# Attention's token-wide products computed in two column halves of the array, beside the state update

## The chip, the cores and the metric

The kernel runs on one core of one Trainium2 chip. The metric is the device time of one execution in microseconds (us); a run gives one time, and the number compared is the median over runs.

## What is computed

Three stages follow each other: an RWKV-like attention, a mixture of eight experts with Sinkhorn gates, and a mixture of eight experts in which each token takes its best one. The change is in the first stage and in two gate products.

```python
def _attn_ref(r, k, v, w, u):            # B=2, H=8 heads, S=768 tokens, D=48
    state = zeros((B, H, D, D))
    for t in range(S):
        cur = einsum('bhd,bhe->bhde', u[None] * kt, vt)
        y[:, :, t] = einsum('bhd,bhde->bhe', rt, state + cur)
        state = wt[:, :, :, None] * state + einsum('bhd,bhe->bhde', kt, vt)
    return y

def _moe_ref(x, w_gate, w1, w2):         # N=1536 tokens, 384 wide, E=8, F=1024
    P = exp(x @ w_gate - max)
    ...                                  # 8 rounds: rows and columns of P scaled
    for e in range(E):
        out += P[:, e:e + 1] * (maximum(x @ w1[e], 0) @ w2[e])

def _moe2_ref(x, expert_emb, tau, w1, w2):
    logits = normalised(x) @ normalised(expert_emb).T / tau
    expert_idx = argmax(logits, axis=1)
    ...                                  # the chosen expert's output, times its softmax weight
```

## The kernel before, in words

The 1536 tokens are 12 chunks of 128, six for each of the two batches. Attention works chunk by chunk in steps, each a Python function that a letter stands for:

- `a` (`att1a`, L579 to L584, VectorE): running products of the decay, and `Rh`, the scaled `r`.
- `b` (`att1b`, L592, L597, VectorE): products from the other side, and `Kt`, the scaled `k`; then loads for the chunk after next.
- `c` (`att1c`, L604 to L609): the part of a token with itself, `bv`; VectorE and, at the end, GpSimd.
- `d` (`att2`): on TensorE the token-by-token products of `Kt` and `Rh` (L620, on two row halves) and four transposes of `Kt` (L623); then VectorE masks them into `AT` (L625), ScalarE copies `KtT` (L630), GpSimd makes `T`, the decayed old state (L633).
- `f` (`att3`): the output of the chunk in one PSUM bank `y`. Four products of `Rh` with `T` (L643, the old state; not in chunks 0 and 6), 96 columns each, and eight of `AT` with the values (L649), 48 columns each; 128 tokens are the stationary columns of both. VectorE adds `bv` into `x` (L655).
- `z` (`att3z`): the state update, eight products of 48 by 48 (L678) that alternate between the lower and the upper column half of the array; VectorE puts them into `S` (L683, L685). The last chunk of a batch, 5 and 11, has no such products.
- `g` (`att4`): three transposes of `x` (L690) and its copies for the experts (L692 to L695).
- `h` (`att5`): three products of the chunk with the gate's weights (L729), eight columns each; ScalarE copies them into `P` (L730).

There is no scheduler: instructions stand on each engine in the order in which the Python code issues them. `run` issues the pieces of an expert unit one by one, and after piece i the steps that stand in slot i of a hand-written string, slots being parted by commas (L1261 to L1264 with the units, the strings' chunks 3 to 11). A unit of 256 tokens has eight hidden pieces (`h_piece`: nine products at L272, ScalarE's `hh`, VectorE's `hl`) and then four output pieces (`y_part`, twelve products each at L292 to L294). Chunks 0 to 2 run before, between the first expert's first chunk and short runs of idle products (`warm`, L522) that keep TensorE busy.

In the third stage `route_mm` (L884) makes three products of a transposed token tile with the expert embeddings, for the tiles 10 and 11 alone.

An fp32 product at these lines is recorded twice, as two weight loads and two multiplies.

Of the kernel before, what the change touches and what calls it, by code (L numbers as in the profile page):

```python
# [19 lines left out]
def rwkv_sinkhorn_moe_top1_moe(  # L20
# [17 lines left out]
    nc = tc.nc  # L38
    B, CPB, _, _, H, D = rkv.shape
    NT, DM = out.shape  # L40
    E, _, FF = m1w1.shape
    NTILE = NT // 128
    KD = DM // 128
# [22 lines left out]
    def ps():  # L66
        return psp.tile([128, 512], F32, tag="ps", name="ps")
# [19 lines left out]
    enT = const.tile([128, KD, E], F32, name="enT")  # L87
    wtab = const.tile([128, E], F32, name="wtab")
    first = const.tile([128, 1], I32, name="first")
# [25 lines left out]
    def xT_of(t0, n):  # L115
        i, o = (0, t0) if t0 < TL else (1, t0 - TL)
        return [t[:, :, o * 128:o * 128 + n] for t in xT_t[i]]
# [179 lines left out]
    def unit_pieces(g, xh, xl, n, finish, nq=2):  # L297
        hts, box = [], []
        pieces = [lambda f=f: h_piece(g, f, xh, xl, n, hts) for f in range(KF)]
        for tl in range(n // 128):  # L300
            for q in range(nq - 1):
                pieces.append(lambda tl=tl, q=q: y_part(g, q, nq, tl, hts, box))

            def last(tl=tl):
                finish(tl, y_part(g, nq - 1, nq, tl, hts, box))

            pieces.append(last)
        return pieces
# [209 lines left out]
    def warm(n):  # L518

        t = ps()  # L520
        for _ in range(n):
            nc.tensor.matmul(t[:, 0:128], oneb, oneb)  # L522
# [18 lines left out]
    Tt = nat.tile([128, HP, 2 * D], F32, name="T")  # L541
    wg8 = acc[0:E, NTILE - 1, 0:DM]
    wgT = nat.tile([128, KD, E], F32, name="wgT")
# [91 lines left out]
    def att3(c):  # L635
        d = st[c]
        first = c % CPB == 0
        vv = vn[c % NB]
        y = ps()
        begin = True  # L640
        if not first:
            for p in range(HP):
                nc.tensor.matmul(  # L643
                    y[:, p * 2 * D:(p + 1) * 2 * D], d["Rh"][0:64 + D, p, :], Tt[0:64 + D, p, :],
                    start=begin, stop=False,
                )
                begin = False
        for h in range(H):
            nc.tensor.matmul(  # L649
                y[:, h * D:(h + 1) * D], d["AT"][:, h % 2, h // 2, :], vv[:, h, :],  # L650
                start=begin, stop=(h == H - 1),
            )
            begin = False
        x = a1.tile([128, DM], F32, tag="x", name="x")
        nc.vector.tensor_tensor(x, y[:, 0:DM], flat(d["bv"]), ALU.add)  # L655
        d["x"] = x
        v_read(c)

    def v_read(c):
        st[c]["reads"] = st[c].get("reads", 0) + 1  # L660
        if st[c]["reads"] == 2:
            att_load_rows(c + NB)
# [61 lines left out]
    def att5(c):  # L724

        xf = st.pop(c)["xf"]
        p = ps()
        for j in range(KD):
            nc.tensor.matmul(p[:, 0:E], xf[:, j, :], wgT[:, j, :], start=(j == 0), stop=(j == KD - 1))  # L729
        nc.scalar.activation(out=P[:, c, :], in_=p[:, 0:E], func=AF.Copy)  # L730


# [43 lines left out]
    def m1_finish(e, t0):  # L776
        def f(tl, p):
            t = t0 + tl
            a = acc[:, t, 0:DM]
            if e == 0:  # L780
                nc.scalar.activation(out=a, in_=p, func=AF.Copy)
            else:
                if e == 1:
                    nc.scalar.mul(a, a, P[:, t, 0:1])
                nc.vector.scalar_tensor_tensor(
                    out=a, in0=p, scalar=P[:, t, e:e + 1], in1=a, op0=ALU.mult, op1=ALU.add
                )
        return f
# [3 lines left out]
    def m1_unit(e, t0, n, nq=2):  # L792
        return unit_pieces(e, *xT_of(t0, n), n, m1_finish(e, t0), nq)
# [86 lines left out]
    def route_mm(t):  # L880
        xT = rr.pop(t)
        p = ps()
        for j in range(KD):
            nc.tensor.matmul(  # L884
                p[:, 0:E], xT[:, j * 128:(j + 1) * 128], enT[:, j, :], start=(j == 0), stop=(j == KD - 1)
            )
        nc.vector.tensor_copy(lg[:, t, :], p[:, 0:E])

    def route_arg(t0, t1):
# [261 lines left out]
    with tc.manual_schedule():  # L1151
# [61 lines left out]
        p = ps()  # L1213
# [8 lines left out]
        split_lo(0, 0)  # L1222
        warm(W2)
        att3(0)
        split_hi(0, 1)
        split_lo(0, 1)
# [12 lines left out]
        def att(text):  # L1239

            steps = {
                "a": att1a, "b": att1b, "c": att1c, "d": att2, "f": att3, "z": att3z, "g": att4, "h": att5,
            }
            return [[lambda w=w: steps[w[0]](int(w[1:])) for w in slot.split()] for slot in text.split(",")]

        def run(pieces, sides):
            for pc, sd in zip(pieces, sides):
                pc()
                for it in sd:
                    it()  # L1250

        def both(x, y):
# [3 lines left out]
            att("a1, b1, z0, h0, , d1, , b2 g1 z1 h1"),  # L1256
            [[gate_T], [], [hi(3), lo(3, nc.gpsimd)], [hi(4), lo(4, nc.gpsimd)], [hi(5)], [hi(6), lambda: warm(W3)],
             [lambda: att1c(1), lo(5), lo(6), lambda: att1a(2), lambda: att3(1)], []],
        ))
        run([lambda: warm(W4)] * 4, att("d2 c2 a3, z2, f2, g2"))  # L1260
        run(m1_unit(0, 1, 256), att("b3, c3 h2, d3, a4, f3, z3 b4, g3 c4, d4 h3, a5, f4, b5, g4 c5 z4"))  # L1261
        run(m1_unit(0, 3, 256), att("d5 h4, a6, f5, z5 b6, g5 c6, h5, d6, a7, f6, z6 b7, g6 c7, h6"))
        run(m1_unit(0, 5, 256), att("d7, a8, f7, z7 b8, g7 c8, h7, d8, a9, f8, z8 b9, g8 c9, d9 h8"))
        run(m1_unit(0, 7, 256), att("a10, f9, z9 b10, g9 c10, d10 h9, a11, f10, z10 b11, g10 c11, d11, f11, g11 z11 h10"))  # L1264
        att_stack.close()
        seven = ExitStack()
        sp0 = ctx.enter_context(tc.tile_pool(name="sp0", bufs=1, side="left", reuse_waits="tile"))
# [6 lines left out]
        h2 = seven.enter_context(tc.tile_pool(name="h2", bufs=4, side="left", reuse_waits="tile"))  # L1274
# [9 lines left out]
        def route(t0, t1, eng):  # L1284
# [12 lines left out]
        S0 = row_sums(0, nc.vector)  # L1297
        run(m1_unit(0, 9, 384, 4), [
            [lambda: att5(NCH - 1), sk[0]] + S0[0:1], [sk[1]] + S0[1:2], [sk[2], sk[3]] + S0[2:4], S0[4:5],
            [sk[4]] + S0[5:6], [sums(0)], [sk[5]] + S0[6:7], [w1[0]] + S0[7:8],  # L1300
            [sk[6]], [], [sums(1)], [sk[7]], [], [w1[1]],
# [109 lines left out]
        def more_stages():  # L1411
            stage[:0] = [flat(en)[:, i * FF:(i + 1) * FF] for i in range(E * DM // FF)]
            load_to(E + SURE)

        m2_slot(0, [
            (0, [lambda: route_mm(10), lambda: route_tr(11), ra[4], more_stages]), (1, [lambda: route_mm(11), ra[5], rb[0], rb[1]] + its[6:7]),
            (3, rb[2:4]), (4, rb[4:]), (5, [lambda: m2_load(1)]), (6, [lambda: m2_load(2)]),
            (10, [overflow]), (14, [lambda: m2_xT(1)]),
# [55 lines left out]
```

## Time and profile before

| | |
|---|---|
| median of 3 runs | 1069.5 us (1069.35 to 1069.74) |
| the profiled execution | 1068.51 us, span 1066.8 us |
| TensorE busy | 1046.4 us, 98% of the span |
| VectorE, ScalarE, GpSimd | 66%, 39%, 19% |
| mean granted TensorE clock | 0.995 |
| attention | from the start to about 175 us of the span |

The span is what the profile covers; the execution's own time has 1.7 us around it. In the profile PE is TensorE's multiply, PEld its weight load, DVE is VectorE, ACT ScalarE, POOL GpSimd and SP the engine that issues most transfers. A group of records is written as one row with its count (x16); its busy time is the union of its records, and the time in brackets is how long the engine had stood idle before it, with what ended that.

### The profile page before, as it was taken

How to read it: one execution, taken by the hardware profiler on the slowest of the kernel's cores; microseconds unless marked ns; L12 is line 12 of the kernel's file. 1: busy time of each engine (PE TensorE's matmuls, PEld its weight loads, DVE VectorE, ACT ScalarE, POOL GpSimd, SP SyncE). 2: the span in 40 equal slices, each digit the busy share in tenths (PEclk: the TensorE clock that was granted, in tenths of full speed). 3: DMA queues.
4: the chain of work that ended last, by engine and by line, in shares of the span. 5: the costliest groups of instructions: out<-in, count | busy, mean ns of one | idle time of the engine just before them, and what ended most of it. 6: DMA issues, size and time to landing. Idle time of an engine off the chain costs nothing.

```text
span 1066.8 us, 17966 instructions
## 1 busy us (share of the span) xinstructions
PE 1046.4 (98%) x6833; PEld 1029.2 (96%) x6833; DVE 702.7 (66%) x1404; ACT 414.8 (39%) x857; POOL 202.3 (19%) x387
## 2 busy tenths in 40 slices
PE   8899999999999999999999999999999999999996
PEld 8899999999999999999999999999999998999996
DVE  7777785766665565566556645655566788987774
ACT  3122223353532343234333323432434545566553
POOL 2210115113010011001000200000144664143111
PEclk9899999999999999999999999999999999999999
DMA  9433220110021022012101101201010314977762
GB/s 258 133 86 93 68 68 2 60 60 1 30 92 66 31 87 99 1 61 60 30 1 54 50 16 30 60 30 60 16 61 1 112 53 142 307 251 240 260 216 89
DMA packets 55774, 91.57 MB, mean 86 GB/s; under 512 B 5355, under 2 KB 47191, under 8 KB 55554
## 3 DMA queue, kind: packets, MB, share of 16 engines
q1 hardware_dynamic: 53056, 85.60, 25.7%
q0 software_dynamic: 2624, 4.75, 1.2%
q8 instruction: 56, 0.92, 0.4%
q14 instruction: 36, 0.29, 0.1%
q10 hardware_dynamic: 2, 0.00, 0.0%
HBM read 80.42 MB, written 13.28 MB: 88 GB/s over the span
## 4 chain that ended last, share of the span: by engine, by line
PE 70%; issue 14%; DVE 7%; POOL 5%; ACT 3%; DMA 1%; POOLq 0%; SPq 0%; DVEq 0%; ACTq 0%
PE ps L499 28%; PE ps L424 24%; PE ps L272 6%; PE ps L649 2%; PE ps L292 2%; PE ps L294 1%; PE ps L293 1%; PE ps L620 1%; POOL tmp L721 1%; DVE ps L714 1%; POOL xs L1090 1%; PE ps L643 1%; POOL out_dram L1136 1%; PE ps L623 1%; DVE keep L435 1%
## 5 line engine op out<-in xcount | busy, mean ns | idle before, releaser
L499 PE MATMUL ps<-wA,hh 128*128 128x384 f32 x864 | 221.5, 337 | 0.4 <-ACT hh L439 0.4
L499 PEld LDWEIGHTS ps<-wA,hh 128*128 128x128 f32 x864 | 156.7, 188 | 1.0 <-ACT hh L439 1.0
L503 DVE SCALAR_TENSOR_TENSOR acc<-ps,Pe,acc 128x384 f32<-128x384 f32 x144 | 88.7, 616 | 101.9 <-PE ps L499 101.4
L430 ACT ACTIVATE keep<-ps 128x384 f32<-128x384 f32 x144 | 70.3, 489 | 209.5 <-PE ps L424 207.7
L499 PE MATMUL ps<-wA,hl 128*128 128x384 f32 x432 | 145.7, 337 | 0.1
L440 DVE SCALAR_TENSOR_TENSOR hl<-keep,hh 128x384 fp32r<-128x384 f32 x144 | 81.5, 566 | 92.1 <-ACT hh L439 92.1
L435 DVE TENSOR_TENSOR keep<-ps,keep 128x384 f32<-128x384 f32 x192 | 106.3, 554 | 41.1 <-PE ps L424 35.1
L230 POOL TENSOR_TENSOR stage<-stage 128x128 f32<-128x128 f32 x96 | 49.6, 538 | 415.3 <-DMA stage<-in_moe_w_dram 413.4
L439 ACT ACTIVATE hh<-keep 128x384 fp32r<-128x384 f32 x144 | 75.6, 525 | 123.7 <-DVE keep L435 123.6
L277 ACT ACTIVATE hh<-ps 128x256 fp32r<-128x256 f32 (+1 forms) x152 | 61.9, 410 | 125.6 <-PE ps L272 121.5
L424 PE MATMUL ps<-xTAhi,wA 128*128 128x384 f32 x396 | 101.7, 338 | 0.2 <-ACT keep L430 0.2
L292 PE MATMUL ps<-wA,hh 128*128 128x384 f32 x264 | 90.4, 342 | 0.1
L278 DVE SCALAR_TENSOR_TENSOR hl<-ps,hh 128x256 fp32r<-128x256 f32 (+1 forms) x152 | 67.7, 455 | 33.6 <-ACT hh L277 30.7
L294 PE MATMUL ps<-wA,hl 128*128 128x384 f32 x264 | 88.5, 335 | 0.0
L293 PE MATMUL ps<-wA,hh 128*128 128x384 f32 x264 | 88.3, 335 | 0.0
L499 PEld LDWEIGHTS ps<-wA,hl 128*128 128x128 f32 x432 | 81.1, 188 | 1.3 <-DVE hl L440 1.3
L256 DVE TENSOR_TENSOR wA<-stage,wA 128x768 fp32r<-128x768 f32 (+2 forms) x65 | 72.7, 1124 | 5.4 <-ACT wA L250 5.0
L499 PE MATMUL ps<-slot,hh 128*128 128x384 f32 x288 | 74.2, 339 | 0.0
L424 PEld LDWEIGHTS ps<-xTAhi,wA 128*128 128x128 f32 x396 | 71.7, 188 | 0.5 <-ACT keep L430 0.5
L250 ACT ACTIVATE wA<-stage 128x768 fp32r<-128x768 f32 (+2 forms) x65 | 60.2, 958 | 25.8 <-POOL stage L230 25.1
L424 PE MATMUL ps<-xTAlo,wA 128*128 128x384 f32 x198 | 66.7, 337 | 0.0
L272 PE MATMUL ps<-xTAhi,wA 128*128 128x256 f32 (+1 forms) x336 | 59.3, 312 | 0.7 <-ACT xTAhi L692 0.6
(312 smaller groups left out, 2133.0 us busy)
## 6 DMA issues: line engine op xcount, KB each, us to landing
stage<-in_moe_w_dram SPq DMA_DIRECT2D x55, 384.0 KB
stage<-in_moe_w_dram SPq DMA_DIRECT2D x19, 512.0 KB
en<-in_moe_w_dram SPq DMA_DIRECT2D x17, 512.0 KB
stage<-in_moe_w_dram SPq DMA_DIRECT2D x28, 256.0 KB
rkv<-in_rkv_dram SPq DMA_DIRECT2D x12, 576.0 KB
en<-in_moe_w_dram SPq DMA_DIRECT2D x18, 384.0 KB
rk<-in_wrk_dram SPq DMA_DIRECT2D x24, 192.0 KB
stage<-in_moe_w_dram SPq DMA_DIRECT2D x28, 128.0 KB
```

The source lines that it names most:

```text
L256: eng.tensor_tensor(out=lo, in0=src, in1=hi.bitcast(F32), op=ALU.subtract)
L272: nc.tensor.matmul(p[:, 0:n], w1_of(g, kk, f)[lo], b[:, kk, :], start=(i == 0), stop=(i == len(mm) - 1))
L292: nc.tensor.matmul(p, hh[:, ts], w2h, start=(f == 0), stop=False)
L293: nc.tensor.matmul(p, hh[:, ts], w2l, start=False, stop=False)
L294: nc.tensor.matmul(p, hl[:, ts], w2h, start=False, stop=(f == KF - 1))
L424: nc.tensor.matmul(t, w, x, start=first_mm and q == 0, stop=q == n - 1, skip_group_check=True,)
L430: nc.scalar.activation(out=t, in_=st_[i][bank][:, 0:384], func=AF.Copy)
L435: nc.vector.tensor_tensor(t, st_[i][bank][:, 0:384], t, ALU.add)
L439: nc.scalar.activation(out=hh, in_=src, func=AF.Relu)
L440: nc.vector.scalar_tensor_tensor(out=hl, in0=src, scalar=0.0, in1=hh.bitcast(F32), op0=ALU.max, op1=ALU.subtract)
L499: nc.tensor.matmul(p, h[:, ts], w, start=n == 0, stop=n == len(mm) - 1)
L503: nc.vector.scalar_tensor_tensor(out=a, in0=p, scalar=P[:, t, e:e + 1], in1=a, op0=ALU.mult, op1=ALU.add)
```

## The change

The output, old-state, gate and route products keep their operands and their sums. Each is now issued as two products, one for the tokens 0 to 63 and one for the tokens 64 to 127, whose results go to the lower and the upper 64 partitions of the bank, that is, to the two column halves of the array. In the order strings of chunks 3 to 11 the state update `z` and the gate product `h` of the chunk before move into the slot of an output `f`, right behind it.

```diff
         y = ps()
-        begin = True
+        halves = [slice(64 * j, 64 * j + 64) for j in range(2)]
         if not first:
             for p in range(HP):
+                for s in halves:
+                    nc.tensor.matmul(
+                        y[s, p * 2 * D:(p + 1) * 2 * D], d["Rh"][0:64 + D, p, s], Tt[0:64 + D, p, :],
+                        start=(p == 0), stop=False,
+                    )
+        for h in range(H):
+            for s in halves:
                 nc.tensor.matmul(
-                    y[:, p * 2 * D:(p + 1) * 2 * D], d["Rh"][0:64 + D, p, :], Tt[0:64 + D, p, :],
-                    start=begin, stop=False,
+                    y[s, h * D:(h + 1) * D], d["AT"][:, h % 2, h // 2, s], vv[:, h, :],
+                    start=(first and h == 0), stop=(h == H - 1),
                 )
-                begin = False
-        for h in range(H):
-            nc.tensor.matmul(
-                y[:, h * D:(h + 1) * D], d["AT"][:, h % 2, h // 2, :], vv[:, h, :],
-                start=begin, stop=(h == H - 1),
-            )
-            begin = False
...
         for j in range(KD):
-            nc.tensor.matmul(p[:, 0:E], xf[:, j, :], wgT[:, j, :], start=(j == 0), stop=(j == KD - 1))
+            for i in range(2):
+                s = slice(64 * i, 64 * i + 64)
+                nc.tensor.matmul(p[s, 0:E], xf[:, j, s], wgT[:, j, :], start=(j == 0), stop=(j == KD - 1))
...
         for j in range(KD):
-            nc.tensor.matmul(
-                p[:, 0:E], xT[:, j * 128:(j + 1) * 128], enT[:, j, :], start=(j == 0), stop=(j == KD - 1)
-            )
+            for i in range(2):
+                nc.tensor.matmul(
+                    p[64 * i:64 * i + 64, 0:E], xT[:, j * 128 + 64 * i:j * 128 + 64 * i + 64], enT[:, j, :],
+                    start=(j == 0), stop=(j == KD - 1),
+                )
...
-        run(m1_unit(0, 1, 256), att("b3, c3 h2, d3, a4, f3, z3 b4, g3 c4, d4 h3, a5, f4, b5, g4 c5 z4"))
-        run(m1_unit(0, 3, 256), att("d5 h4, a6, f5, z5 b6, g5 c6, h5, d6, a7, f6, z6 b7, g6 c7, h6"))
-        run(m1_unit(0, 5, 256), att("d7, a8, f7, z7 b8, g7 c8, h7, d8, a9, f8, z8 b9, g8 c9, d9 h8"))
-        run(m1_unit(0, 7, 256), att("a10, f9, z9 b10, g9 c10, d10 h9, a11, f10, z10 b11, g10 c11, d11, f11, g11 z11 h10"))
+        run(m1_unit(0, 1, 256), att("b3, c3, d3, a4, f3 z3 h2, b4, g3 c4, d4, a5, f4 z4 h3, b5, g4 c5"))
+        run(m1_unit(0, 3, 256), att("d5, a6, f5 z5 h4, b6, g5 c6, , d6, a7, f6 z6 h5, b7, g6 c7, "))
+        run(m1_unit(0, 5, 256), att("d7, a8, f7 z7 h6, b8, g7 c8, , d8, a9, f8 z8 h7, b9, g8 c9, d9"))
+        run(m1_unit(0, 7, 256), att("a10, f9 z9 h8, b10, g9 c10, d10, a11, f10 z10 h9, b11, g10 c11, d11, f11 h10, g11 z11"))
```

How the strings move the instructions is seen at two places. The first is TensorE around the output of chunk 3, the first in such a unit: L272 is a hidden piece, L729 the gate product of chunk 2, L620 and L623 step `d` of chunk 3, L643 and L649 its old state and output, L678 its state update. Before:

```order
L729 MATMUL ps<-wgT,acc 128x8 x3
L272 MATMUL ps<-xTAhi,wA 128x256 x6
L272 MATMUL ps<-xTAlo,wA 128x256 x3
L620 MATMUL ps<-Rh,Kt 128x128 x8
L623 MATMUL ps<-ident,Kt 128x128 x4
...
L643 MATMUL ps<-T,Rh 128x96 x4
L649 MATMUL ps<-rkv_132,AT 128x48 x8
L272 MATMUL ps<-xTAhi,wA 128x256 x6
L272 MATMUL ps<-xTAlo,wA 128x256 x3
L678 MATMUL ps<-rkv_132,KtT 48x48 x8
```

In the changed kernel:

```order
L272 MATMUL ps<-xTAhi,wA 128x256 x6
L272 MATMUL ps<-xTAlo,wA 128x256 x3
L620 MATMUL ps<-Rh,Kt 128x128 x8
L623 MATMUL ps<-ident,Kt 128x128 x4
...
L644 MATMUL ps<-T,Rh 64x96 x8
L650 MATMUL ps<-rkv_132,AT 64x48 x16
L678 MATMUL ps<-rkv_132,KtT 48x48 x8
L731 MATMUL ps<-wgT,acc 64x8 x6
L272 MATMUL ps<-xTAhi,wA 128x256 x6
```

The gate product no longer stands ahead of L620, and output, state update and gate are one block of column halves, with twice as many products at the first and the last.

The second place is VectorE around the state update of chunk 4: L655 is its `x`, L685 the state's copy into `S`, L592 and L597 make `Kt` of chunk 5, L605 and L607 belong to its step `c`.

```order
 L655 TENSOR_TENSOR x<-ps,bv 128x384
+L685 TENSOR_TENSOR S<-ps,T 48x4x48 x2
 L592 SCALAR_TENSOR_TENSOR suf<-w_135,seg 128x516
 L597 TENSOR_TENSOR Kt<-rk_130,suf 128x512
...
 L605 TENSOR_TENSOR rkv_132<-rkv_132 128x384
 L607 TENSOR_REDUCE b<-rkv_132 128x8
-L685 TENSOR_TENSOR S<-ps,T 48x4x48 x2
 L278 SCALAR_TENSOR_TENSOR hl<-ps,hh 128x256
```

The copy into `S` moves ahead of the next chunk's `Kt`. In the other chunks of that stretch it moves ahead of one `hl` (L278) and stood ahead of `Kt` before. On SP one load of rows goes ahead of the two pairs of loads for `w` and `rk` of a chunk.

## Rows read from the trace of the kernel before

**Rows 1.** The page, part 1: busy us (share of the span) and instructions.
```profile
PE 1046.4 (98%) x6833; PEld 1029.2 (96%) x6833; DVE 702.7 (66%) x1404; ACT 414.8 (39%) x857; POOL 202.3 (19%) x387
```

**Rows 2.** Busy time by stage: stretch, its us, engines, granted clock, DMA, GB/s.
```profile
53.00:175.00 122.00, 120.93 (x1058) 115.92 (x1058) 87.97 (x175) 30.24 (x77) 20.27 (x67) 1.00 0.24 69
81.60:96.90 15.30, 15.30 (x145) 14.76 (x144) 13.48 (x28) 4.98 (x13) 2.46 (x3) 1.00 0.38 116
39.00:45.80 6.80, 6.80 (x62) 6.23 (x61) 4.61 (x9) 0.60 (x1) 2.52 (x2) 0.50 0.59 161
```

**Rows 3.** TensorE's longest wait in total: for whom, us, times, longest one.
```profile
PE ps L690 <- DVE x L655: 2.2, 2, 2.1
```

**Rows 4.** Records of five lines: count, ns min/median/max, first and last start us.
```profile
L643 PE MATMUL ps<-T,Rh x80: 246/275/474, 29.2 to 167.0; 112*128 112x96 f32 x80
L649 PEld LDWEIGHTS ps<-rkv,AT x192: 187/192/192, 13.8 to 168.7; 128*128 128x128 f32 x192
L729 PEld LDWEIGHTS ps<-wgT,acc x72: 186/192/192, 23.4 to 174.3; 128*128 128x128 f32 x72
L884 PEld LDWEIGHTS ps<-enT,xT x12: 186/192/192, 890.8 to 893.4; 128*128 128x128 f32 x12
L678 PEld LDWEIGHTS ps<-rkv,KtT x160: 119/125/196, 22.6 to 157.7; 128*48 128x48 f32 x160
```

**Rows 5.** Weight loads in order of time, 59 to 75 us: start, busy us, instruction.
```profile
62.14 0.44 PEld L678 LDWEIGHTS ps<-rkv,KtT 128*48 128x48 f32 x16
72.95 1.87 PEld L649 LDWEIGHTS ps<-rkv,AT 128*128 128x128 f32 x16
```

**Rows 6.** Multiplies of two lines, columns as in rows 4.
```profile
L678 PE MATMUL ps<-rkv,KtT x160: 208/208/316, 22.6 to 157.7; 128*48 128x48 f32 x160
L1214 PE MATMUL ps<-u_sb,ones x2: 481/533/585, 6.4 to 6.8; 1*128 1x384 f32 x2
```

**Rows 7.** TensorE in order of time, 57 to 64 us, chunk 3's output and state.
```profile
57.20 0.87 PE L272 MATMUL ps<-xTAhi,wA 128*128 128x256 f32 x6
...
58.27 1.07 PE L643 MATMUL ps<-T,Rh 112*128 112x96 f32 x8
...
60.90 0.96 PE L272 MATMUL ps<-xTAhi,wA 128*128 128x256 f32 x6
...
62.15 0.56 PE L678 MATMUL ps<-rkv,KtT 128*48 128x48 f32 x16
...
63.81 0.49 PE L690 MATMUL ps<-ident,x 128*128 128x128 f32 x3
```

**Rows 8.** Order of time at chunk 1's `x` and its transposes.
```profile
35.53 0.55 DVE L655 TENSOR_TENSOR x<-ps,bv 128x384 f32<-128x384 f32 x1
...
36.14 0.55 PE L690 MATMUL ps<-ident,x 128*128 128x128 f32 x3 [2.05 <-DVE x L655]
```

**Rows 9.** Order of time at chunk 0's `x`.
```profile
15.89 0.56 DVE L655 TENSOR_TENSOR x<-ps,bv 128x384 f32<-128x384 f32 x1 [0.49 <-PE ps L649]
```

**Rows 10.** Order of time from the gate of chunk 2 to `d` of chunk 3.
```profile
52.56 0.73 PE L729 MATMUL ps<-wgT,acc 128*128 128x8 f32 x6
...
53.14 0.95 PE L272 MATMUL ps<-xTAhi,wA 128*128 128x256 f32 x6
...
53.71 0.69 DVE L597 TENSOR_TENSOR Kt<-rk,suf 128x512 f32<-128x512 f32 x1
...
54.55 1.16 PE L620 MATMUL ps<-Rh,Kt 48*128 48x128 f32 x16
```

**Rows 11.** Order of time at chunk 10: its `AT` and its output.
```profile
151.93 1.28 DVE L625 TENSOR_TENSOR AT<-ps,mask 128x512 f32<-128x512 f32 x2
...
153.56 1.03 PE L643 MATMUL ps<-T,Rh 112*128 112x96 f32 x8
```

**Rows 12.** Order of time at chunk 6: its `Kt` and its `d`.
```profile
92.00 0.69 DVE L597 TENSOR_TENSOR Kt<-rk,suf 128x512 f32<-128x512 f32 x1
...
94.24 0.94 PE L620 MATMUL ps<-Rh,Kt 48*128 48x128 f32 x12
```

## The prediction

> **What bounds the kernel now.** I read the engine totals first: TensorE is busy 98% of the span, VectorE 66% [rows 1], so time leaves this kernel only where TensorE gets less to do and nothing else takes its place. The table by stage comes next: between 53 and 175 us, where chunks 3 to 11 of attention run inside the first expert's products, TensorE is busy 120.93 of 122.00 us and VectorE 87.97; in a stretch where the first expert's hidden pieces run (81.6 to 96.9 us) VectorE has 13.48 of 15.30; from 39.0 to 45.8 us the granted clock is 0.50, the 1.2 GHz level [rows 2]. The list of TensorE's waits is short: at its head stand 2.2 us in all for `x` [rows 3]. So a microsecond taken from attention's products is a microsecond of the kernel, except where one of those waits, or one just behind it, swallows it.
>
> **What a product costs.** Each fp32 product is two records, a weight load and a multiply each. The old-state line has 80 records, the output line 192, the gate line 72, the route's line 12 [rows 4]. The output line loads 128 columns of weights per record; its 16 loads last 1.87 us together, one load 0.192, so they follow each other every (1.87 − 0.192) / 15 = 0.1119 us, though only 48 columns move through. The state update, before and after on 48-column halves, has 16 loads in 0.44 us, one lasting 0.125: eight pairs, one every (0.44 − 0.125) / 7 = 0.0450 us [rows 4, 5]. Two points give 0.836 ns per weight column, so a pair of 64-column halves should come every 0.0584 us if the load sets the pace. After the change every record of 128 columns is one such pair: 0.0535 us less.
>
> The multiply sets the pace where more columns move. An fp32 record lasts 481 ns with 384 moving columns (the shorter of two) and 208 with 48 [rows 6]: 0.81 ns per column. A state-update pair (48 moving) is then 39 + 6 ns; the old-state pair (96 moving) 78 + 6 = 84 ns. The trace shows no old-state pair: 58.4 ns (load alone) and 84 ns (multiply) are its ends, 111.9 the present; I take 84, because the two multiply rows are of this data type. Gain 0.0279.
>
> - Output: 192 × 0.0535 = 10.27 us.
> - Gate: 72 × 0.0535 = 3.85 us. Route: 12 × 0.0535 = 0.64 us.
> - Old state: 80 × 0.0279 = 2.23 us (4.28 at the other end).
>
> Together 17.0 us. The Trainium skill (TensorE: Matmul & The Clock Gate, section Part 3: Packing small matmuls) gives a measured 2.38 times for three column tiles; the same yield per tile would be 1.59 times for two, a pair every 70.4 ns, and by that estimate the sum would be 13.7 us, not 17.0. The state update's pairs in this trace, 45.0 ns, do not show such a loss.
>
> **What entering and leaving the halves costs.** Two hidden pieces with a state update between them take 60.90 to 63.81 = 2.91 us; the same piece alone takes 57.20 to 58.27 = 1.07 [rows 7]. The update costs 2.91 − 2.14 = 0.77, of which eight pairs are 0.36: 0.41 us per block of halves. A state update already pays this; output and gate put beside it pay nothing more. New blocks are those that do not touch a state update: output of chunks 0, 1, 2; gate of 0 and 11; the route's products of tiles 10 and 11; and the blocks of chunks 5 and 11, which have no state product. Nine × 0.41 = 3.69 us. That leaves 13.3 us.
>
> **What of it is on the path.** Three places give it back:
> - Output of chunk 1, with its old state, gets 16 × 0.0535 + 8 × 0.0279 − 0.41 = 0.67 us shorter, but its `x` starts at 35.53 with VectorE at work without a pause before it, and TensorE stands 2.05 us for it [rows 8]. Minus 0.67. Chunk 0's gain stays: there `x` waited for TensorE [rows 9].
> - Gate 2 now runs at 52.56 to 53.14, ahead of a product that starts at 54.55 when `Kt` (53.71 + 0.69) is ready [rows 10]. Moved behind output 3, it no longer covers that wait: minus 0.6, the 0.58 it filled.
> - Gate 9 leaves the place before output 10, whose `AT` is ready only 0.35 us ahead (151.93 + 1.28 against 153.56) [rows 11]: minus 0.4. The same with gate 4 before output 5, where the room is larger: minus 0.2.
>
> Other moves I cost at nothing. The state's copy into `S`, 0.71 us of VectorE, now comes ahead of a `hl` and, for chunk 4, ahead of the next `Kt`; but its product also ends a piece earlier, and `Kt` 6 was ready at 92.69 for a product at 94.24, 1.55 us of room [rows 12]. Without that room each such move costs 0.71. The gate's 0.18 us copy on ScalarE has nobody waiting before the normalisation. One row load on SP goes ahead of two others; the chunk that reads it is two chunks away. But TensorE leaves about 11 of the 122 us of this stage while VectorE keeps its 88, so its share goes from 72% to 79%; I put 0.6 us on small new waits. The bounds of this term are 0 and the second rival below.
>
> Sum: 13.3 − 0.7 − 0.6 − 0.6 − 0.6 = 10.8 us. The profiled execution took 1068.5 us, a span of 1066.8 and 1.7 around it; less 10.8 it is 1057.7. The median of the runs shown, 1069.5, is 1.0 above it, so the median after is **1058.7 us**. Old state at its good end and no new waits give 1069.5 − 10.8 − 2.05 − 0.6 = 1056.0; if half the price of a block were the tail of the work before it, 1.8 less: 1054.2.
>
> **The rivals.**
> 1. *VectorE becomes the bound in the hidden-piece stretches.* For: 13.48 of 15.30 us [rows 2], and TensorE's work there shrinks by over 1 us. Against: the 1.55 us of room [rows 12], and VectorE starts such a stretch with work ahead of it. Outputs 3, 5, 7, 9 and 10 lie in such stretches; each block's 0.86 + 0.22 + 0.32 = 1.4 us would turn into waits, 7.0 in all, instead of the 1.8 I took off for waits and moved gates there: 1058.7 + 5.2 = 1063.9. Chance 0.15.
> 2. *The low clock lasts longer.* It stood at 0.50 for 6.8 us [rows 2], after TensorE had idled 2.05 us and worked thinly [rows 8]; that idle time grows by 0.67. A second stretch as long would do 3.4 us of full-clock work in 6.8: 1058.7 + 3.4 = 1062.1. Against: some of that stretch waits for VectorE anyway. Chance 0.10.
> 3. *Slower: the two halves of one product load one after the other.* They share their moving operand, which the state update's halves do not. Then a pair takes 2 × 58.4 = 116.8 ns: 276 × 4.9 ns = 1.35 us more for output, gate and route; the old state 2 × 84 = 168 ns, 80 × 56 ns = 4.5 more; with 3.69 for the blocks, 9.5 us: 1079. It decides from about 96 ns a pair, where 356 × 16 ns no longer pays the blocks and the 1.9 us of covered places. Against: 45.0 ns for a pair of 48 columns is what one load takes by the per-column rate, so two ran at once [rows 5]. Chance 0.05. The Trainium skill (same page and section) states a rule that points this way: a weight load overlaps a running multiply only if it uses other rows of the array, and both halves use the same rows. The trace does not agree for 48 columns; no run here shows 64.
> 4. *No change:* switching costs 1.5 us a block where new, not 0.41, and nine of them eat the 13.3 + 3.69 − 1.9 us: about 1068. The state update inside hidden pieces speaks against it [rows 7]. Chance 0.04.
>
> **How the numbers follow.** My forecast has 0.66 (own range 1054.8 to 1061). The range reaches over rival 2 and about half of rival 1: 1055.0 to 1064.5; outside lie the upper part of rival 1, rivals 3 and 4 and the best end. About 0.2% (2.1 us) is what a measurement can tell from no change. Faster: 0.66 + 0.15 + 0.10 = 0.91; same: 0.04; slower: 0.05.
>
> **What would show it.** In the profile after: output records with 64 columns whose 32 loads last about 16 × 58 ns + 0.1 = 1.0 us instead of 1.87; 16 old-state loads in about 0.7 us; no separate state-update block between two hidden pieces of the long stretch; TensorE's wait for `x` 1 near 2.7 us, for `Kt` 3 near 0.9, and a new wait of some tenths at output 10; VectorE's 88 us unchanged in a stage of about 112. I am wrong on the pace if pairs come slower than 70 ns; on the path if the stage from 53 us shortens by less than 7 us while its products shrink as told; on the clock if the 0.50 stretch is longer than 7 us.

## The result, and the profile after

The changed kernel takes 1057.1 us (median of four runs, 1056.5 to 1057.6) where the kernel before took 1069.6 beside it: a ratio of 0.9883 (95% interval 0.9866 to 0.9901), 12.5 us less. The forecast was 1058.7, in a range from 1055.0 to 1064.5. The profiled execution was the slowest of the four, 1057.64 us.

The page's first part, engine totals, answers to [rows 1]:

```profile
PE 1033.5 (98%) x7189; PEld 1014.1 (96%) x7189; DVE 701.8 (66%) x1404; ACT 415.1 (39%) x857; POOL 199.3 (19%) x387
```

TensorE has 356 records more (6833 to 7189, one for each of the 356 that were split) and 12.9 us less work. VectorE has what it had. To see where the time went I cut both traces at the same instructions: the start of the token-by-token products `d` of chunks 0, 1 and 3, and the transposes of chunk 11.

| stretch | before, us | after, us | change | forecast |
|---|---|---|---|---|
| start to `d` 0 | 10.81 | 10.32 | −0.49 | 0 |
| `d` 0 to `d` 1 | 13.94 | 13.32 | −0.62 | −0.36 |
| `d` 1 to `d` 3 | 29.80 | 30.13 | +0.33 | −1.06 |
| `d` 3 to transposes of chunk 11 | 116.49 | 106.41 | −10.08 | −9.02 |
| rest | 895.76 | 895.75 | −0.01 | −0.40 |

(The last column regroups the prediction's terms by place.) Nearly everything was won in the long stretch, more than forecast. Between `d` 1 and `d` 3 nothing was won at all in this profile. The first line waits for loads, which the change doesn't touch: VectorE's first step starts when `w` has come, at 5.39 us before and at 4.97 after.

Busy time by stretch (columns as in [rows 2]), `d` 1 to `d` 3 and the long stretch of the kernel before:

```profile
24.75:54.55 29.80, 26.44 (x243) 24.23 (x242) 22.41 (x42) 7.37 (x17) 8.04 (x6) 0.89 0.51 141
54.55:171.04 116.49, 115.58 (x1019) 110.85 (x1020) 85.45 (x171) 27.86 (x69) 16.46 (x63) 1.00 0.25 72
```

And of the changed kernel, with a piece of the first that is read further down:

```profile
23.64:53.77 30.13, 25.57 (x290) 22.32 (x289) 22.70 (x43) 7.26 (x16) 8.06 (x6) 0.83 0.53 148
49.50:52.90 3.40, 3.40 (x16) 3.30 (x16) 1.84 (x4) 0.71 (x2) 0.00 (x0) 0.50 0.00 0
53.77:160.18 106.41, 104.82 (x1294) 99.75 (x1294) 83.71 (x170) 28.63 (x71) 16.90 (x64) 1.00 0.28 79
```

In the long stretch TensorE's busy time fell by 10.76 us, from 115.58 to 104.82, and its idle time rose from 0.91 to 1.59. VectorE now has 83.71 of 106.41 us, 79%, the forecast share, and the stretch is still TensorE's. In the first stretch TensorE has less work and the time is the same: the mean granted clock fell from 0.89 to 0.83, and the idle time grew.

The pace of the products shows in the weight loads, 55 to 75 us, in order of time (the rows answer to [rows 5]):

```profile
57.58 0.69 PEld L644 LDWEIGHTS ps<-T,Rh 112*64 112x64 f32 x16
58.22 1.04 PEld L650 LDWEIGHTS ps<-rkv,AT 128*64 128x64 f32 x32
59.17 0.45 PEld L678 LDWEIGHTS ps<-rkv,KtT 128*48 128x48 f32 x16
59.53 0.44 PEld L731 LDWEIGHTS ps<-wgT,acc 128*64 128x64 f32 x12
```

and their single durations in the rows of two lines (columns as in [rows 4]):

```profile
L644 PEld LDWEIGHTS ps<-T,Rh x160: 132/137/137, 28.1 to 156.5; 112*64 112x64 f32 x160
L731 PEld LDWEIGHTS ps<-wgT,acc x144: 133/138/227, 22.5 to 163.4; 128*64 128x64 f32 x144
```

Output: 32 loads are 16 pairs, (1.04 − 0.138) / 15 = 60 ns a pair. Gate: (0.44 − 0.138) / 5 = 60 ns. Old state: (0.69 − 0.137) / 7 = 79 ns. The state update is as it was. The same place on TensorE, which answers to [rows 7]:

```profile
56.43 0.88 PE L272 MATMUL ps<-xTAhi,wA 128*128 128x256 f32 x6
...
57.59 0.88 PE L644 MATMUL ps<-T,Rh 112*64 112x96 f32 x16
58.30 1.09 PE L650 MATMUL ps<-rkv,AT 128*64 128x48 f32 x32
59.22 0.53 PE L678 MATMUL ps<-rkv,KtT 128*48 128x48 f32 x16
59.58 0.49 PE L731 MATMUL ps<-wgT,acc 128*64 128x8 f32 x12
59.99 0.98 PE L272 MATMUL ps<-xTAhi,wA 128*128 128x256 f32 x6
```

Old state, output, state update and gate of a chunk are one block of 59.99 − 57.59 = 2.40 us. Before, old state and output alone took 60.90 − 58.27 = 2.63 [rows 7].

TensorE's waits (us in total, times, longest one):

```profile
PE ps L690 <- DVE x L655: 3.6, 3, 2.2
PE ps L620 <- DVE Kt L597: 1.5, 3, 0.8
PE ps L272 <- ACT xTAhi L692: 1.2, 2, 0.6
...
PE ps L272 <- ACT xTBhi L692: 0.6, 1, 0.6
...
PE ps L644 <- POOL T L633: 0.3, 1, 0.3
```

The wait for `x` grew from 2.2 to 3.6 us [rows 3]. In order of time, at chunks 1 and 2:

```profile
34.43 0.55 DVE L655 TENSOR_TENSOR x<-ps,bv 128x384 f32<-128x384 f32 x1
35.03 0.55 PE L690 MATMUL ps<-ident,x 128*128 128x128 f32 x3 [2.17 <-DVE x L655]
...
38.47 2.08 PE L620 MATMUL ps<-Rh,Kt 48*128 48x128 f32 x16
...
47.50 0.55 PE L690 MATMUL ps<-ident,x 128*128 128x128 f32 x3 [1.26 <-DVE x L655]
48.63 0.97 PE L272 MATMUL ps<-xTAhi,wA 128*128 128x256 f32 x6 [0.58 <-ACT xTAhi L692]
```

From `d` 1 (23.64) to the transposes of chunk 1 (35.03) are 11.39 us; before they were 36.14 − 24.75 = 11.39 too [rows 8]. Old state and output 1 became shorter, and nothing of that reached the end. Behind chunk 2 TensorE idles 1.26 and 0.58 us, and 0.9 us later the granted clock is at 0.50, the 1.2 GHz level, for 3.4 us (49.5 to 52.9, above). This is the second such stretch; the first stands from 35.9 to 42.7.

### The profile page after: what moved, and what is told of

It is laid out like the page before. It is cut to its first block, busy times and chain, and to the rows that moved or that the text cites. A ratio compares the mean times of both kernels' runs of the same rounds, so it can differ in the third digit from the quotient of the medians.

```text
span 1055.9 us, 18668 instructions
## 1 busy us (share of the span) xinstructions
PE 1033.5 (98%) x7189; PEld 1014.1 (96%) x7189; DVE 701.8 (66%) x1404; ACT 415.1 (39%) x857; POOL 199.3 (19%) x387
## 5 line engine op out<-in xcount | busy, mean ns | idle before, releaser
L278 DVE SCALAR_TENSOR_TENSOR hl<-ps,hh 128x256 fp32r<-128x256 f32 (+1 forms) x152 | 67.7, 454 | 26.9 <-ACT hh L277 25.3
L272 PE MATMUL ps<-xTAhi,wA 128*128 128x256 f32 (+1 forms) x336 | 59.7, 314 | 1.2 <-ACT xTAhi L692 1.2
```

The lines of the kernel that those rows point to most:

```text
L272: nc.tensor.matmul(p[:, 0:n], w1_of(g, kk, f)[lo], b[:, kk, :], start=(i == 0), stop=(i == len(mm) - 1))
```

## Experiments

Two questions were open: what the split gives and what the placement gives in the long stretch, and why the stretch from `d` 1 to `d` 3 gave nothing. Each run has the kernel before beside it; its medians there lay between 1068.9 and 1069.2 us. Where no edit is told, a kernel is the changed one.

**Split alone and placement alone.** The first kernel keeps the split products and has the four order strings of before; the second has the products of before and the new strings.

```diff
-        run(m1_unit(0, 1, 256), att("b3, c3, d3, a4, f3 z3 h2, b4, g3 c4, d4, a5, f4 z4 h3, b5, g4 c5"))
+        run(m1_unit(0, 1, 256), att("b3, c3 h2, d3, a4, f3, z3 b4, g3 c4, d4 h3, a5, f4, b5, g4 c5 z4"))
...
```

> All products split as in the change, but the order strings of before. Theory (a pair of halves every 58 ns, and a fixed price for each block of halves that stands apart): 16 blocks more than in the changed kernel (35 against 19). At the 0.41 us of the prediction they cost 6.6 us, at the 0.28 us that I read from the changed kernel's trace 4.5; the gate products back at their old places cover waits again, worth about 1.2. So 3.3 to 5.4 us above the changed kernel's 1057.1: 1060.4 to 1062.5. Rival (the placement is worth nothing, the split all): 1057. Rival (the placement is worth it, the split little): about 1069.

> The order strings of the change, no product split. Theory: the state update is the only block of halves, as before, so nothing is saved; gates 2, 4 and 9 no longer cover the waits for Kt 3, output 5 and output 10, which costs up to 1.2 us: 1069.6 to 1070.8. Rival (the earlier state update frees VectorE's Kt sooner and that is where time came from): 1066 or less.

Split alone: 1060.5 us, ratio 0.9928 (0.9914 to 0.9941). Placement alone: 1070.2, ratio 1.0016 (1.0007 to 1.0025), 1.7 us slower by the ratio. So the split by itself gives 8.4 us by the medians. The changed kernel is 12.1 to 12.5 us below the kernel before in the three comparisons of the two, so the new order adds some 3.7 to 4.0; with the old products it only costs. What it costs are three places from which a product went that had filled a wait, in order of time on TensorE:

```profile
54.25 1.01 PE L620 MATMUL ps<-Rh,Kt 48*128 48x128 f32 x13 [0.76 <-DVE Kt L597]
```

```profile
81.04 0.97 PE L272 MATMUL ps<-xTAhi,wA 128*128 128x256 f32 x6 [0.64 <-ACT xTAhi L692]
```

```profile
173.62 1.31 PE L272 MATMUL ps<-xTBhi,wA 128*128 128x384 f32 x6 [0.63 <-ACT xTBhi L692]
```

TensorE stands 0.76 us for `Kt` 3, where gate 2 ran before [rows 10]; 0.64 for the copy of chunk 4's transposes, where state update 4 ran; 0.63 for that of chunk 11's, where gate 10 ran. The three are 2.0 us, of the order of what the run lost (1.3 us by the medians, 1.7 by the ratio). The prediction has the first of them only.

What a block costs to enter and leave is read from the long stretch of the first kernel (columns as in [rows 2]):

```profile
53.26:162.70 109.44, 108.52 (x1269) 100.49 (x1270) 84.91 (x171) 27.71 (x69) 16.57 (x63) 1.00 0.28 77
```

It has 23 blocks of column halves there (nine outputs, seven gates, seven state updates), the changed kernel nine. TensorE is busy 108.52 against 104.82 us, 3.70 more, although gates 2 and 10 lie outside: 12 pairs of 58.4 ns, 0.70. That is 4.40 / 14 = 0.31 us a block. One place shows it singly:

```profile
57.78 1.09 PE L650 MATMUL ps<-rkv,AT 128*64 128x48 f32 x32
58.80 0.97 PE L272 MATMUL ps<-xTAhi,wA 128*128 128x256 f32 x6
...
60.06 0.56 PE L678 MATMUL ps<-rkv,KtT 128*48 128x48 f32 x16
60.55 0.98 PE L272 MATMUL ps<-xTAhi,wA 128*128 128x256 f32 x6
```

From the hidden piece that follows an output (58.80) to the next one (60.55) are 1.75 us, of which a piece alone is 1.07 [rows 7]: the separate state update adds 0.68, beside the output it adds 59.58 − 59.22 = 0.36. Of the 0.32 between them some may be the piece's own: behind a different instruction pieces of this trace also take up to 1.15.

**One product made whole again.** First the gate, then the old state.

```diff
-            for i in range(2):
-                s = slice(64 * i, 64 * i + 64)
-                nc.tensor.matmul(p[s, 0:E], xf[:, j, s], wgT[:, j, :], start=(j == 0), stop=(j == KD - 1))
+            nc.tensor.matmul(p[:, 0:E], xf[:, j, :], wgT[:, j, :], start=(j == 0), stop=(j == KD - 1))
```

> The changed kernel with the attention's gate products whole again (128 columns), the order as changed. Theory: 72 records of 111.9 ns in place of pairs of 58.4, 3.85 us, less the two blocks of gates 0 and 11 that go (0.6 to 0.8): 3.1 us above the changed kernel, 1060.2. Rival (gate products lie beside VectorE's work and their length is hidden): within 1 us of 1057.1.

```diff
-                for s in halves:
-                    nc.tensor.matmul(
-                        y[s, p * 2 * D:(p + 1) * 2 * D], d["Rh"][0:64 + D, p, s], Tt[0:64 + D, p, :],
-                        start=(p == 0), stop=False,
-                    )
+                nc.tensor.matmul(
+                    y[:, p * 2 * D:(p + 1) * 2 * D], d["Rh"][0:64 + D, p, :], Tt[0:64 + D, p, :],
+                    start=(p == 0), stop=False,
+                )
```

> The changed kernel with the old-state products whole again, ahead of the split output in the same place. Theory (an old-state pair is paced by its 96 moving columns, 84 to 88 ns): 80 records at 111.9 ns, 1.9 to 2.2 us longer, of which chunk 1's 0.2 is hidden: 1.7 to 2.0 above, 1058.8 to 1059.1. Rival (the weight load paces it, 58 ns): 4.1 above, 1061.2. Rival (hidden behind VectorE): 1057.

Gate whole: 1060.4 us, ratio 0.992 (0.9907 to 0.9934). Old state whole: 1059.8, ratio 0.9913 (0.9899 to 0.9926). Their long stretches, in this order, against 106.41:

```profile
53.70:163.38 109.68, 108.10 (x1240) 102.74 (x1241) 83.89 (x171) 28.20 (x70) 17.27 (x64) 1.00 0.27 77
```

```profile
53.69:162.01 108.32, 106.73 (x1230) 102.21 (x1230) 83.88 (x171) 28.57 (x71) 16.91 (x64) 1.00 0.27 78
```

Nine whole gates cost 3.27 us there, 6 × 9 × 0.0535 = 2.89 of it by the pairs; the rest may be the change between whole products and halves within a block, which this kernel has and the changed one has not. So the gate's length is on the path. The old state costs 108.32 − 106.41 = 1.91 us over 8 chunks of 8 records: 29.8 ns a record, a pair of 111.9 − 29.8 = 82 ns. The multiply's price (84) holds, the load's (58.4) falls. The run as a whole lost more than the 1.7 to 2.0 us expected: its median is 2.6 us above the 1057.1 of the changed kernel. TensorE's busy time in the stretch rose by the same 1.91 us (106.73 against 104.82), so the price is taken from there.

**The stretch from `d` 1 to `d` 3.** Theory: TensorE idles 2.17 us for `x` 1, and the low clock follows; at the low clock all of chunk 2 comes later. Rival: VectorE's own order makes `x` 2 late (step `a` of chunk 3 stands ahead of it), whatever the clock. The runs fill the wait with idle products, move `a` 3 behind output 2, and do both, beside the changed kernel itself.

```diff
-            att("a1, b1, z0, h0, , d1, , b2 g1 z1 h1"),
+            att("a1, b1, z0, h0, , d1, , b2 w36 g1 z1 h1"),
```

```diff
-        run([lambda: warm(W4)] * 4, att("d2 c2 a3, z2, f2, g2"))
+        run([lambda: warm(W4)] * 4, att("d2 c2, z2, f2 a3, g2"))
```

(`w36` issues 36 of the idle products.)

> The changed kernel itself, for a comparison on the same chip. The kernel before took 1068.9 us on the chip of the last four runs, 0.6 below the first measurement, so this should be near 1056.5, with a profile that again shows a stretch of 6.8 us at clock 0.50 and at times another of 3.4 us.

> The changed kernel with 36 idle products (2.0 us) put where TensorE stands 2.2 us for chunk 1's x. Theory (the low clock that follows that idle time is paid by TensorE's work from 37 to 53 us): the granted clock stays at 1.00 there, step d of chunk 2 takes 1.2 in place of 2.1 us, the hidden pieces after 48 us run at the full clock: 1.6 to 3 us below the changed kernel. Rival (VectorE's order alone sets the pace of that stretch): within 0.5 us of it, though the clock is 1.00.

> The changed kernel with step a of chunk 3 (2.8 us of VectorE) behind output 2 in place of ahead of it. Theory (the split made output 2 ready at 45.6 while its x starts at 46.9 because VectorE is at step a): x of chunk 2 starts 1.3 us sooner, and so the hidden pieces: 1.0 to 1.3 us below the changed kernel. Rival (step a is then late for chunk 3): no gain or slower.

> Both edits of the two runs before. If both theories hold: 2.5 to 4 us below the changed kernel, the sum of the two, less what they share (less idle time at the clock's fall). If only one holds, that one's gain.

| kernel | median, us | ratio, interval | `d` 1 to `d` 3 | granted clock 0.50 (start, us) |
|---|---|---|---|---|
| changed, again | 1056.7 | 0.9885 (0.9868 to 0.9901) | 30.17 | 36.1, 6.8; 49.8, 3.4 |
| idle filled | 1056.8 | 0.9893 (0.9876 to 0.9909) | 28.45 | 46.4, 3.4 |
| `a` 3 moved | 1058.2 | 0.9902 (0.9886 to 0.9919) | 30.21 | 34.5, 10.2 |
| both | 1055.8 | 0.9872 (0.9855 to 0.9888) | 27.43 | 48.5, 3.4 |

(The last two columns are of one profiled execution each.) Filling the wait did take the first low stretch away, and the time of the run stayed. The idle time had only moved, to `x` 2:

```profile
45.50 0.55 PE L690 MATMUL ps<-ident,x 128*128 128x128 f32 x3 [1.99 <-DVE x L655]
```

and behind it stands a low stretch:

```profile
46.40:49.80 3.40, 3.17 (x15) 3.17 (x16) 0.99 (x3) 0.94 (x3) 0.00 (x0) 0.50 0.01 5
```

Moving `a` 3 alone gained nothing; its median is 1.4 us above the changed kernel's. In that profile the clock stood at 0.50 for 10.2 us (34.50:44.70), output 2 came at 45.62 instead of 44.48, and the first hidden piece behind it at 48.57 instead of 48.63. Behind that `x` TensorE waits for VectorE again, 0.90 us for `xTAlo`, which now comes after `a` 3, and 0.76 for `Kt` 3:

```profile
50.44 0.62 PE L272 MATMUL ps<-xTAlo,wA 128*128 128x256 f32 x3 [0.90 <-DVE xTAlo L695]
```

So neither theory is right by itself. With the idle time filled, VectorE's order holds the end of the stretch; with `a` 3 moved, the longer low stretch and VectorE's later steps take back what `x` 2 wins (8.52 us in place of 9.03 from `d` 2 to the transposes of chunk 2). Both together took 1.0 us off the median, not the 2.5 to 4 expected. What they gave in the stage (27.43) is partly hidden in that profile by 2 us more between `d` 0 and `d` 1 (15.39): ScalarE stood 1.52 us for a transfer of expert weights there, and TensorE 1.96 us for ScalarE's next copy.

**The order of VectorE around `x` 2.** In the changed kernel VectorE has this in order of time there:

```profile
43.43 1.22 DVE L579 TENSOR_TENSOR_SCAN Q<-w,seg 128x516 f32<-128x516 f32 x1
...
46.14 0.71 DVE L685 TENSOR_TENSOR S<-ps,T 48x192 f32<-48x192 f32 x2
46.88 0.56 DVE L655 TENSOR_TENSOR x<-ps,bv 128x384 f32<-128x384 f32 x1
...
52.66 0.69 DVE L597 TENSOR_TENSOR Kt<-rk,suf 128x512 f32<-128x512 f32 x1
```

Step `a` 3 runs from 43.43 to 46.1, the output's products have ended by 45.6, and `x` 2 starts at 46.88; `Kt` 3 (step `b` 3), for which TensorE also waits, comes 5.8 us behind it. Three kernels: idle filled and `b` 3 moved ahead into the slot of output 2; `b` 3 alone so; and idle filled with `x` 2 ahead of both, `a` 3 behind output 2 and `b` 3 behind its transposes. The first and the last as diffs (the second is the first without the filling):

```diff
+            att("a1, b1, z0, h0, , d1, , b2 w36 g1 z1 h1"),
...
-        run([lambda: warm(W4)] * 4, att("d2 c2 a3, z2, f2, g2"))
-        run(m1_unit(0, 1, 256), att("b3, c3, d3, a4, f3 z3 h2, b4, g3 c4, d4, a5, f4 z4 h3, b5, g4 c5"))
+        run([lambda: warm(W4)] * 4, att("d2 c2 a3, z2, f2 b3, g2"))
+        run(m1_unit(0, 1, 256), att(", c3, d3, a4, f3 z3 h2, b4, g3 c4, d4, a5, f4 z4 h3, b5, g4 c5"))
```

```diff
+            att("a1, b1, z0, h0, , d1, , b2 w36 g1 z1 h1"),
...
+        run([lambda: warm(W4)] * 4, att("d2 c2, z2, f2 a3, g2 b3"))
+        run(m1_unit(0, 1, 256), att(", c3, d3, a4, f3 z3 h2, b4, g3 c4, d4, a5, f4 z4 h3, b5, g4 c5"))
```

> The changed kernel again, for the comparison on this chip: 1056.5 to 1057. In its profile, from step d of chunk 1 to step d of chunk 3 about 30.1 us, and from there to the transposes of chunk 11 about 106.4, as in its two profiles so far; the kernel before has 29.8 and 116.5.

> Idle products before chunk 1's transposes as in the run with the idle time filled, and step b of chunk 3 behind output 2, ahead of the copies of chunk 2, in place of behind the first hidden piece. Theory (from the first to the third step d VectorE sets the pace, and the split of outputs 1 and 2 gains nothing there until VectorE's order follows it): Kt 3 is ready at about 47.5, step d of chunk 3 starts when three hidden pieces are done, 27 to 28 us after that of chunk 1 in place of 30.1: 2 to 3 us below the changed kernel. Rival (that stretch is not on the path to the end): no gain.

> The same move of step b without the idle products. Theory (the low clock is then what is left): the hidden pieces behind chunk 2 run at the low clock in part, as in the changed kernel, and last as long as Kt 3 did: 0 to 0.7 us below the changed kernel. Rival (Kt 3 alone was the bound): 1.5 us below or more.

> Idle products as before, chunk 2's x as soon as output 2 is there, then step a of chunk 3, the copies of chunk 2, step b of chunk 3. Theory: the hidden pieces start 2 us sooner than with the idle time filled alone, wait once for the low part of chunk 2 behind step a, and step d of chunk 3 starts 26 to 27 us after that of chunk 1: 3 to 4 us below the changed kernel. Rival (VectorE's work up to Kt 3 is the same sum in any order): as the run with step b early, within 0.5 us.

| kernel | median, us | ratio, interval | `d` 1 to `d` 3 | granted clock 0.50 (start, us) |
|---|---|---|---|---|
| changed, third time | 1057.0 | 0.989 (0.9873 to 0.9906) | 28.89 | 37.5, 6.8 |
| idle filled, `b` 3 early | 1056.0 | 0.9882 (0.9866 to 0.9899) | 28.41 | 47.4, 3.4 |
| `b` 3 early | 1057.1 | 0.9887 (0.9871 to 0.9904) | 28.60 | 37.1, 6.8 |
| `x` 2 first, idle filled | 1053.9 | 0.9856 (0.984 to 0.9872) | 25.91 | none |

The first two edits moved nothing that can be told from the changed kernel's own spread (the first 1.0 us, where 2 to 3 were expected). The last one took 3.1 us off it, and its slowest run (1054.6) is below the fastest of the changed kernel (1056.4). Behind the transposes of chunk 11, where none of the runs of this and the last comparison has an edit, their profiles take 895.5 to 897.0 us; a gain of less than that difference shows in the stage rather than in the total. Its stretch and the place at chunk 2:

```profile
23.54:49.45 25.91, 23.36 (x326) 20.41 (x325) 22.49 (x43) 7.14 (x16) 7.21 (x6) 1.00 0.58 165
```

```profile
43.17 0.56 DVE L655 TENSOR_TENSOR x<-ps,bv 128x384 f32<-128x384 f32 x1 [0.82 <-PE ps L650]
43.78 0.55 PE L690 MATMUL ps<-ident,x 128*128 128x128 f32 x3
...
46.78 0.62 PE L272 MATMUL ps<-xTAlo,wA 128*128 128x256 f32 x3 [0.89 <-DVE xTAlo L695]
```

The clock stays at 1.00 and VectorE waits for TensorE at `x` 2, not the reverse. Part of the wait returns at `xTAlo`, 0.89 us, which VectorE now makes behind the moved steps. VectorE's busy time is as it was (22.49 us, 22.41 before): only its order and the clock changed. Which part of the 3.1 us needs the filling is not shown, for this order was not run without it.

The third profile of the changed kernel, meanwhile, has one low stretch, like the kernel before:

```profile
23.76:52.65 28.89, 24.34 (x291) 20.97 (x290) 22.43 (x42) 7.63 (x17) 8.05 (x6) 0.88 0.53 149
```

Against 30.13 and 30.17 us in the two profiles with a second stretch it is 1.25 us shorter, and 0.9 shorter than before. (The kernel with the split products and the old strings has one low stretch too, and 28.90 us.) About half of the 1.25 lies at the second stretch. The third profile on TensorE, in order of time:

```profile
35.16 0.55 PE L690 MATMUL ps<-ident,x 128*128 128x128 f32 x3 [2.19 <-DVE x L655]
...
38.00 2.08 PE L620 MATMUL ps<-Rh,Kt 48*128 48x128 f32 x16
...
47.03 0.55 PE L690 MATMUL ps<-ident,x 128*128 128x128 f32 x3 [0.37 <-DVE x L655]
```

From the transposes of chunk 1 to `d` 2 it takes 2.84 us, in the first profile 38.47 − 35.03 = 3.44; from `d` 2 to the transposes of chunk 2 9.03 both times; from there to `d` 3 5.62 and 6.27. So 0.60 us go where the first low stretch starts, at 35.9 and 36.1 us in place of 37.5 (gate 1 takes 0.81 in place of 0.52 us), and 0.65 behind chunk 2, where the second one stands. The other profiles show the same pattern. Where the first stretch starts by 36.1 us (these two; `a` 3 moved; the gate whole and the old state whole, 35.7 and 35.5), the clock is low for 10.2 us in all, in one piece or in two. Where it starts at 37.1 or later (the kernel before; the third profile; `b` 3 early; split alone and placement alone, 38.1 and 37.9), it is low for 6.8. No run shows what moves that start.

## Why the prediction was right, and where it was off

The total was right, 1.6 us above the median and well inside the range. The profiled execution, on which the sum was made, shows less of a miss: 1068.51 − 10.8 = 1057.7 was forecast for it and 1057.64 came, but by errors that cancel. So it is luck that the profiled execution came out so near. Runs of one kernel differ by 1 to 2 us: the medians lie 12.5 us apart and the profiled executions 10.9, because that of before was below its median and that of after above.

- *The price of a pair.* Forecast 58.4 ns, measured 60 (output and gate); old state 84, measured 79 in the loads and 82 by the run with it whole. Both per-column rates held: the load paces what moves 48 columns or fewer, the multiply what moves 96. With the measured paces the 17.0 us would be 16.7.
- *Halves side by side* (rival 3). The rival fell: pairs of 60 ns are half of the 116.8 that two loads one after the other would take. The rule quoted there, from the Trainium skill (TensorE: Matmul & The Clock Gate, section Part 3: Packing small matmuls), that a weight load overlaps a running multiply only if it uses other rows, doesn't hold for these halves, which use the same rows and other columns. The estimate from the same section's 2.38 times for three column tiles, 70.4 ns a pair, was too slow: 111.9 / 60 is 1.87 times for two.
- *The price of a block* was the term mis-sized in the long stretch: 0.41 us forecast, 0.31 as the runs have it. The piece of 1.07 us that I took off was one that followed another piece directly; behind other instructions it takes 1.15, and what I booked on the block was partly that. By itself it explains little of the stretch: with nine blocks instead of seven, and 0.10 less for each of the two new ones, 0.2. TensorE's busy time fell by 10.76 where the terms give 10.22 (pairs 11.74, less gates 2 and 10, 0.70, and two blocks, 0.82). With the measured paces of the pairs and 0.31 for a block the terms give 10.2 again, so 0.5 us of it I can't place. Between `d` 0 and `d` 1, where two more of the new blocks lie, the smaller price makes −0.56 of the forecast's −0.36; −0.62 was measured.
- *No new waits for VectorE* (rival 1). The 0.6 us put on small waits did not come, nor the 0.2 at output 5. VectorE went to 79% of the stretch as forecast and stayed ahead. At output 10 a wait came, 0.28 instead of 0.4, but for `T`, which GpSimd makes, where I had named `AT`:

```profile
143.99 0.88 PE L644 MATMUL ps<-T,Rh 112*64 112x96 f32 x16 [0.28 <-POOL T L633]
```

- *A cover I did not see.* I asked who waits behind gate 2, 4 and 9, but not what the state update 4 covered. Before, it ran between the transposes of chunk 4 and the first hidden piece that reads them:

```profile
79.02 0.49 PE L690 MATMUL ps<-ident,x 128*128 128x128 f32 x3
79.44 0.56 PE L678 MATMUL ps<-rkv,KtT 128*48 128x48 f32 x16
80.14 0.97 PE L272 MATMUL ps<-xTAhi,wA 128*128 128x256 f32 x6
```

  Now it stands with output 4, and ScalarE's copy of the transposes is waited for:

```profile
76.66 0.49 PE L690 MATMUL ps<-ident,x 128*128 128x128 f32 x3
77.78 0.97 PE L272 MATMUL ps<-xTAhi,wA 128*128 128x256 f32 x6 [0.63 <-ACT xTAhi L692]
```

  From the transposes to the piece it is 1.12 us both times: the 0.77 us that leaving should have given here (0.36 for the pairs, the rest for the block) gave nothing. Gate 10, moved away from the end of chunk 11, leaves the same wait for `xTBhi` (0.6 in the list of waits), which takes up the 0.4 us forecast for the rest. These two were fillers, as gate 2 was. Idle time in the long stretch rose by 0.68 us where I had 1.2, so this error hid behind the VectorE waits that didn't come.
- *Output 1 and gate 2* (the 0.67 and 0.6 us on the path). Output 1 gave exactly nothing, as forecast, but not by the one wait I named: that for `x` grew only from 2.05 to 2.17, not to 2.7. Most went into the piece behind output 1, which takes 2.65 us from its first to its last product where it took 2.00, and now meets the expert's weights `wA` before VectorE has them ready:

```profile
31.72 0.44 PE L293 MATMUL ps<-wA,hh 128*128 128x384 f32 x1 [0.16 <-DVE wA L256]
```

  Before, there was no such wait there. `Kt` 3 is waited for 0.76 us, where I had 0.9, in the profile with one low stretch; in the other two TensorE comes late itself.
- *The low clock* (rival 2) came true in two of three profiles of the changed kernel: a second stretch, 3.4 us long, beside the 6.8 as before. The rival had a second 6.8 us at a price of 3.4, half of its length; the 3.4 us that came cost 0.65, not 1.7, and the counter-argument there, that some of such a stretch waits for VectorE anyway, would account for most of the difference: the 0.76 us for `Kt` 3 stand in the third profile alone. Another 0.60 us came from the first stretch, by its earlier start, which no rival had. My sign for being wrong on the clock was a 0.50 stretch longer than 7 us: no single one was in the changed kernel, but the two together are 10.2. The stage `d` 1 to `d` 3, forecast at −1.06, changed by +0.33, +0.38 and −0.91 in three profiles; so the step that failed there is the one that took the clock's stretch as it was before. With one low stretch output 2 gave 0.92 (from `d` 2 to the transposes of chunk 2, 9.95 before and 9.03 after; 0.67 was forecast), and gate 1, forecast at 0.32, nothing (2.85 and 2.84 from the transposes of chunk 1 to `d` 2).

How the second stretch comes about stays partly open. In the profiles each low stretch follows a place where TensorE idles or works thinly, and filling one place moved the stretch to the next; but the same kernel shows it in two profiles and not in a third, where the idle time ahead of chunk 2's transposes was 0.37 instead of 1.26 us. Which of the two is the cause was not tried separately.

## What to carry to other kernels

A small fp32 product whose weight loads set the pace gets nearly twice as fast by two column halves; price it by the load and the multiply rate of two rows, and take the larger. Put the halves beside other halves, for each separate block costs some 0.3 us, but look at each product that is moved for what waits behind the place it leaves: it may have been the filler. Where a stage waits for VectorE, a shorter product gives nothing there; the order of VectorE's steps did here, together with idle products in TensorE's idle time.

## What the runs showed of the hardware that was not expected

- Between `d` 1 and `d` 3 the granted clock of one and the same kernel falls differently from execution to execution: 0.50 for 6.8 and 3.4 us, or for 6.8 alone; the kernel with `a` 3 moved shows 10.2 in one piece. With that goes a difference of 1.25 us in the stage, which no edit explains.
- Two column halves on the same rows work at once: 60 ns a pair of 64-column loads with the same moving operand, 45 ns [rows 5] with 48 columns.
